# The last FFN by halves of its hidden width, and a second value group in columns form, in a four-layer decode kernel

## The chip, the cores and the metric

The kernel runs on one core of one Trainium2 chip. The metric is the device time of one execution in microseconds (us). PE is the matmul engine, PEld its weight loads, DVE the vector engine, ACT the scalar engine, SP the engine that issues the loads. "Clock" is the share of its full clock that PE was granted.

## The reference, cut to what matters

Two attention layers with a key and value cache and two gated FFNs alternate, for one new token of each of four sequences:

```python
B, Sq, D = 4, 1, 512
Hq, Hkv, Sk, Dh = 32, 8, 8192, 128        # caches: 4 x 8 x 8192 x 128, bf16, two of them
F = 1792
def _B_ref(x, w_gate, w_up, w_down):
    g = _silu(x @ w_gate)
    u = x @ w_up
    return (g * u) @ w_down
x = x + _A_ref(_layernorm(x), ...)        # attention
x = x + _B_ref(_layernorm(x), ...)        # FFN
x = x + _A_ref(_layernorm(x), ...)
x = x + _B_ref(_layernorm(x), ...)
```

The two caches hold 134 MB and are needed by both attention layers. The kernel keeps little of them on the chip and loads most of them twice: some 257 MB in all, the weights included.

## The kernel before

Everything is a step of a plan. A small simulation inside the kernel (`Plan.run`) assigns each step a start by estimated durations, and the program is then emitted in that order. Three rules of it matter here: which step an engine takes, how the estimate of a PE step grows when its instruction stream crosses a block of 256, and that a group's output projection (`oproj`) ranks by the place of the group's second load.

```python
# Plan.run: of the steps of one engine, the one ready when it comes free; ties by prio
at = max(t, free_at[e])
k = (at > free_at[e] + 1e-9, at if at > free_at[e] + 1e-9 else 0.0, s.prio[0])
...
# Plan.run.fetched: an estimate of instruction fetch, at most one block of 256 per 6 us
for k in range(first // self.PAGE_N + 1, pe_n // self.PAGE_N + 1):
    there = at + s.us * (k * self.PAGE_N - first) / s.n
    at += max(0.0, page_at + self.PAGE - there)
    page_at = max(there, page_at + self.PAGE)
```

A value group multiplies the softmax weights by two loads of 1 MB of values. In rows form that is 16 matmuls of 256 columns per load, then a 128x256 transpose and a reduction on DVE. In columns form it is 32 matmuls of 4 columns per load, and the result needs neither.

```python
direct = (l, b, g) in late_groups          # LATE = (6, ): group 6, last sequence, last attention
# rows:    matmul(out[32n:32n+32, 0:256], lhsT=p[:, 32 columns], rhs=v[:, 8 rows, 32 of 128])
# columns: matmul(out[:, 0:4],            lhsT=v[:, 128 of one row], rhs=p[:, 4 columns])
def nm():
    if not direct:
        e.transpose(blk, blk); e.tensor_reduce(osum[:], diag, AX.X, ALU.add)
    e.tensor_tensor(oT[...], got, invL[...], ALU.mult)
...
return prev, oproj(l, g, [n, ...], prios[1])
```

The FFN: 56 gate matmuls, two times 28 up matmuls, then silu over the whole width, the product with each half of up, and two times 28 down matmuls.

```python
gate = ffn_mm(wg_sb, "wg", 0, FO, [cen], tag + "g")              # FO = 14, 4 matmuls each
ups = [...]                                                      # two halves
# a1 gs = gate * rstd            DVE
# a2 eneg = exp(-gs)             ACT
# a3 us = gs * rstd              DVE
# a4 us = us / (1 + eneg)        DVE: add, reciprocal, multiply
# a5 hT[half] = us[half] * up[half]   DVE, twice
# dn: 28 down matmuls for each half
```

## Time and profile before

| | before |
|---|---|
| median of the first 3 runs | 640.53 us (639.56 to 641.21) |
| profiled span | 637.9 us |
| loads | 257 MB, 403 GB/s, DMA row at 9 or 8 in 39 of 40 slices |
| from the last long load wait to the end | 624.11 to 637.9, 13.8 us |

The lines of the page and of the timeline that carry this stand in the prediction below. They are read in two steps: the stream of loads up to about 624 us, and what PE and DVE still have to do after that. I call that stretch the tail.

- **A**: from the end of the last long load wait on PE to the first add after the projections (before: 624.11 to 628.70, 4.59 us),
- **B**: from the first gate matmul to the first down matmul (630.26 to 633.74, 3.48 us),
- **C**: from that wait's end to the end of the last vector copy (624.11 to 635.99 + 0.21 = 636.20, 12.09 us).

Two lines of DVE's timeline in the kernel before, which the prediction doesn't show: the last step of the value group's result in rows form, and the first add.

```profile
627.43 0.17 DVE L777 TENSOR_TENSOR oT<-osum,invL 128x4 bf16<-128x4 f32 x1
628.70 0.17 DVE L861 TENSOR_TENSOR xx<-xx,ps 128x16 f32<-128x16 f32 x1 [0.90 <-PE ps L709]
```

### The profile page before, as it was taken

The page shows a single profiled execution, that of the slowest core. Times are in us where ns is not written, and L with a number is a line of the kernel's source. Part 1 is how long each engine was busy: PE and PEld are TensorE (multiplying, and loading weights), DVE is VectorE, ACT ScalarE, POOL GpSimd, SP SyncE. Part 2 cuts the span into 40 slices and gives each one's busy share as a digit, 9 for nine tenths or more (in the row PEclk, how much of TensorE's full clock was granted, in tenths as well). Part 3 has the DMA queues.
Part 4 walks back from the last instruction along what each step waited for, and adds up shares of the span by engine and source line. Part 5 has one row for each costly group of instructions (what it writes and reads, how often), then busy time and mean ns, then how long its engine had stood idle before and what let it go on. Part 6 is the DMA issues. An engine that isn't in the chain of part 4 may idle for free.

```text
span 637.9 us, 18599 instructions
## 1 busy us (share of the span) xinstructions
PE 401.5 (63%) x8657; PEld 202.0 (32%) x8657; DVE 405.2 (64%) x612; ACT 40.2 (6%) x106; POOL 1.8 (0%) x8
## 2 busy tenths in 40 slices
PE   0376454375686655678565575677656776866676
PEld 0231221123542131145331241343421244721355
DVE  6386853464236958776579765466667864499732
ACT  1000200002000020000100100000100020000200
POOL 1000000000000000000000000000000000000000
PEclk9985585565556686665677677567585578577685
DMA  8999999999989999999999999999999999999991
GB/s 362 420 418 407 407 418 420 418 421 400 388 354 422 420 418 420 421 418 404 417 414 418 420 419 421 419 409 411 417 420 420 403 420 420 420 416 420 421 415 42
DMA packets 41124, 257.31 MB, mean 403 GB/s; under 512 B 3924, under 2 KB 9816, under 8 KB 11096
## 3 DMA queue, kind: packets, MB, share of 16 engines
q1 hardware_dynamic: 41048, 256.14, 97.8%
q8 instruction: 67, 1.10, 0.7%
q14 instruction: 9, 0.07, 0.0%
HBM read 256.12 MB, written 0.00 MB: 402 GB/s over the span
## 4 chain that ended last, share of the span: by engine, by line
DMA 64%; PE 16%; DVE 13%; SPq 3%; issue 2%; ACT 0%
DMA pool<-in_A_k_cache_dram 45%; DMA pool<-in_A_v_cache_dram 12%; DVE pool L589 9%; PE ps L605 8%; DMA wq_sb<-in_A_k_cache_dram 5%; PE ps L746 4%; SPq L92 3%; DMA wq_sb<-in_A_v_cache_dram 3%; PE ps L467 1%; DVE negm L624 1%; DVE wq_sb L589 1%; PE ps L792 1%; PE ps L664 1%; PE ps L845 1%; DVE ps L773 1%
## 5 line engine op out<-in xcount | busy, mean ns | idle before, releaser
L589 DVE STREAM_TRANSPOSE pool<-pool 128x2048 uint32<-128x2048 uint32 x116 | 267.1, 2308 | 88.4 <-DMA pool<-in_A_k_cache_dram 87.9
L605 PE MATMUL ps<-pool,qpad 32*32 32x512 bf16 x3840 | 197.4, 548 | 130.8 <-DVE pool L589 125.6
L605 PEld LDWEIGHTS ps<-pool,qpad 32*32 32x32 bf16 x3840 | 55.5, 110 | 248.4 <-DVE pool L589 185.8
L746 PE MATMUL ps<-pool,pp 128*32 128x256 bf16 x1952 | 100.5, 362 | 37.6 <-DMA pool<-in_A_v_cache_dram 28.9
L746 PEld LDWEIGHTS ps<-pool,pp 128*32 128x32 bf16 x1952 | 56.2, 120 | 76.3 <-DMA pool<-in_A_v_cache_dram 34.9
L773 DVE STREAM_TRANSPOSE ps<-ps 128x256 f32<-128x256 f32 x63 | 28.8, 457 | 67.4 <-PE ps L746 67.1
L628 ACT ACTIVATE pp<-ps,negm 128x512 bf16<-128x512 f32 x32 | 21.6, 686 | 322.8 <-DVE negm L624 300.5
L709 PE MATMUL ps<-oT,wo_sb 128*128 128x4 bf16 x640 | 22.4, 166 | 11.3 <-DVE oT L777 8.4
L709 PEld LDWEIGHTS ps<-oT,wo_sb 128*128 128x128 bf16 x640 | 20.0, 102 | 24.8 <-DVE oT L777 15.8
L624 DVE TENSOR_REDUCE negm<-ps 128x1 f32<-128x512 f32 x32 | 19.9, 683 | 12.4 <-PE ps L605 12.4
L467 PE MATMUL ps<-xnT,wq_sb 128*128 128x4 bf16 x640 | 18.3, 166 | 12.8 <-DMA wq_sb<-in_A_wq_dram 11.5
L467 PEld LDWEIGHTS ps<-xnT,wq_sb 128*128 128x128 bf16 x640 | 17.7, 104 | 15.3 <-DMA wq_sb<-in_A_wq_dram 11.6
L589 DVE STREAM_TRANSPOSE wq_sb<-wq_sb 128x2048 uint32<-128x2048 uint32 x8 | 18.5, 2312 | 1.8 <-DMA wq_sb<-in_A_k_cache_dram 1.8
L605 PE MATMUL ps<-wq_sb,qpad 32*32 32x512 bf16 x256 | 11.8, 492 | 9.1 <-DVE wq_sb L589 9.1
L664 PE MATMUL ps<-ident,pp 128*128 128x128 bf16 x128 | 15.4, 300 | 2.5 <-DVE oT L777 1.1
L453 ACT ACTIVATE lnv<-var,eps_sb 128x4 f32<-128x4 f32 x10 | 3.0, 297 | 221.5 <-DVE var L448 221.5
L664 PEld LDWEIGHTS ps<-ident,pp 128*128 128x128 bf16 x128 | 11.9, 137 | 9.6 <-DVE selw L684 2.9
L775 DVE TENSOR_REDUCE osum<-ps 128x4 f32<-128x32 f32 x63 | 12.1, 192 | 2.2
L777 DVE TENSOR_TENSOR oT<-osum,invL 128x4 bf16<-128x4 f32 x63 | 10.6, 169 | 2.1
L673 ACT ACTIVATE pp<-ps 128x1024 bf16<-128x1024 bf16 x8 | 8.2, 1024 | 30.1 <-PE ps L664 30.1
L845 PE MATMUL ps<-hT,wd_sb 128*128 128x4 bf16 x280 | 8.6, 166 | 1.8 <-issue 1.1
L653 DVE TENSOR_SCALAR pp<-pp,alpha 128x512 bf16<-128x512 bf16 x32 | 9.0, 344 | 1.1 <-ACT alpha L646 1.1
(68 smaller groups left out, 143.4 us busy)
## 6 DMA issues: line engine op xcount, KB each, us to landing
pool<-in_A_k_cache_dram SPq DMA_DIRECT2D x116, 1024.0 KB, 10.2
pool<-in_A_v_cache_dram SPq DMA_DIRECT2D x101, 1024.0 KB, 10.8
wq_sb<-in_A_k_cache_dram SPq DMA_DIRECT2D x8, 1024.0 KB, 14.8
wq_sb<-in_A_v_cache_dram SPq DMA_DIRECT2D x5, 1024.0 KB, 16.2
wq_sb<-in_A_wq_dram SPq DMA_DIRECT2D x1, 4096.0 KB, 20.0
wo_sb<-in_A_wo_dram SPq DMA_DIRECT2D x4, 1024.0 KB, 15.5
wg_sb<-in_B_w_gate_dram SPq DMA_DIRECT2D x2, 896.0 KB, 19.2
wu_sb<-in_B_w_up_dram SPq DMA_DIRECT2D x2, 896.0 KB, 16.9
```

The source lines that it names most:

```text
L92: ins = self.eng[engname].dma_start(out_ap, in_ap)
L467: op("pe", lambda e: e.matmul(ps[:, bk * BW + h * B:bk * BW + (h + 1) * B], lhsT=wq_sb[:, kt, h * Dh:(h + 1) * Dh], rhs=xnT[:, kt * B:(kt ...
L589: op("dve", lambda e: e.transpose(v, v), reads=keys, writes=keys)
L605: op("pe", lambda e: e.matmul(ps[32 * c:32 * (c + 1), a * BW:(a + 1) * BW], lhsT=qpad[rows, qbuf, es_, g, :], rhs=ap[h][rows, :, es_ // 2, ...
L624: op("dve", lambda e: e.tensor_reduce(negm[:, q, a:a + 1], bank(a), AX.X, ALU.max, negate=True), reads=[f"pb{a}"], writes=[f"negm{q}_{a}"])
L628: op("act", lambda e: e.activation(pblk(q)[:, :, a, :], bank(a).rearrange("p (t j) -> p t j", j=32), ACTF.Exp, bias=negm[:, q, a:a + 1], s ...
L664: op("pe", lambda e: e.matmul(stg[:, t * P:(t + 1) * P], lhsT=pp[:, q, blk * P:(blk + 1) * P], rhs=ident[:], is_transpose=True, start=True ...
L709: op("pe", lambda e: e.matmul(ps[:, OPJ * BW + nq * B:OPJ * BW + (nq + 1) * B], lhsT=wo_sb[:, h, nq * P:(nq + 1) * P], rhs=oT[:, l, h, :], ...
L746: op("pe", lambda e: e.matmul(ps[32 * n:32 * (n + 1), bk * BW:bk * BW + 256], lhsT=pp[:, q, col:col + 32], rhs=v[:, 8 * f:8 * (f + 1), 32 ...
L773: op("dve", lambda e: e.transpose(blk, blk), reads=[f"pb{bk}"], writes=[f"pb{bk}"])
L775: op("dve", lambda e: e.tensor_reduce(osum[:], diag, AX.X, ALU.add), reads=[f"pb{bk}"], writes=["osum"])
L845: op("pe", lambda e: e.matmul(ps[:, bk * BW + nq * B:bk * BW + (nq + 1) * B], lhsT=wd_sb[:, fo, nq * P:(nq + 1) * P], rhs=hT[:, fo * B:(fo ...
```

## The change

Its intent: let the last FFN's silu begin when half of the gate is there, so that it is finished when PE comes to the down projection; and spare a further late value group the transpose and reduction after its matmuls.

```diff
-LATE = (6, )
+LATE = (6, 3)
...
-            gate = ffn_mm(wg_sb, "wg", 0, FO, [cen], tag + "g")
+            parts = 2 if dst is not None else 1        # dst: the last FFN only
+            for k in range(parts):
+                gates.append(ffn_mm(wg_sb, "wg", k * FO // parts, (k + 1) * FO // parts,
+                                    [cen] + gates[-1:], f"{tag}g{k}"))
...
+            for k in range(parts):
+                cs = slice(k * FO * B // parts, (k + 1) * FO * B // parts)
                 # a1, a2, a3, a4 as before, on columns cs alone
+                silu.append(PL.add("dve", 0.98 if parts == 1 else 0.65, a4, [e_, r_], CHAIN))
...
-                hs_ = PL.add("dve", 0.2, a5, [s, ups[h]], CHAIN, free=f"{tag}u{h}")
+                hs_ = PL.add("dve", 0.2, a5, [silu[h * parts // 2], ups[h]], CHAIN, free=f"{tag}u{h}")
```

## The prediction

> **What bounds the kernel now.** I read the page from the top: engine shares and slices, the DMA queue, the chain that ended last, and then, because the diff touches only the end of the program, the timeline of the last 30 us.
>
> ```profile
> PE 401.5 (63%) x8657; PEld 202.0 (32%) x8657; DVE 405.2 (64%) x612; ACT 40.2 (6%) x106; POOL 1.8 (0%) x8
> DMA  8999999999989999999999999999999999999991
> q1 hardware_dynamic: 41048, 256.14, 97.8%
> DMA 64%; PE 16%; DVE 13%; SPq 3%; issue 2%; ACT 0%
> ```
>
> No compute engine is above 64%, the DMA row is at 9 from the second slice to the last but one, and the data queue fills 97.8% of the span. 257 MB at 403 GB/s is the kernel; nothing that the diff does before the last load lands can be worth anything. The last DMA slice (622 to 638) reads 1, so there is a compute tail there. Its timeline and the waits say what it consists of:
>
> ```profile
> 619.49 0.55 PE L709 MATMUL ps<-oT,wo_sb 128*128 128x4 bf16 x16
> 624.11 1.05 PE L746 MATMUL ps<-wq_sb,pp 128*32 128x256 bf16 x16 [4.07 <-DMA wq_sb<-in_A_v_cache_dram]
> 625.09 0.59 PE L709 MATMUL ps<-oT,wo_sb 128*128 128x4 bf16 x16
> 625.61 1.04 PE L746 MATMUL ps<-pool,pp 128*32 128x256 bf16 x16
> 626.59 1.01 PE L731 MATMUL ps<-pp,pool 128*128 128x4 bf16 x32
> 627.65 1.01 PE L709 MATMUL ps<-oT,wo_sb 128*128 128x4 bf16 x32
> 629.13 0.64 PE L433 MATMUL ps<-xx,onesm 128*128 128x32 f32 x2 [0.47 <-DVE xx L428]
> 630.26 1.65 PE L792 MATMUL ps<-xnT,wg_sb 128*128 128x4 bf16 x56 [0.49 <-DVE xnT L442]
> 631.78 1.63 PE L792 MATMUL ps<-xnT,wu_sb 128*128 128x4 bf16 x56
> 633.74 1.65 PE L845 MATMUL ps<-hT,wd_sb 128*128 128x4 bf16 x56 [0.33 <-DVE hT L837]
> ```
>
> PE waits 4.07 us for a value load (one of the last three), then works almost without a gap to the end. From 624.11 to the span's end at 637.9 are 13.8 us, 2.2% of the span. That is all the change can work on. In it PE is the bound; its own idle time is 0.47 and 0.49 us around the layer norm (untouched) and 0.33 us in front of the down projection, named in the waits as DVE hT.
>
> ```profile
> 631.95 0.22 DVE L812 TENSOR_TENSOR gs<-ps,rstd 128x56 f32<-128x56 f32 x1 [1.48 <-PE ps L792]
> 632.21 0.25 ACT L817 ACTIVATE eneg<-gs 128x56 f32<-128x56 f32 x1 [1.16 <-DVE gs L812]
> 632.49 0.19 DVE L826 TENSOR_SCALAR eneg<-eneg 128x56 f32<-128x56 f32 x1
> 632.71 0.50 DVE L828 RECIPROCAL eneg<-eneg 128x56 f32<-128x56 f32 x1
> 633.25 0.22 DVE L829 TENSOR_TENSOR us<-us,eneg 128x56 f32<-128x56 f32 x1
> 633.50 0.28 DVE L837 TENSOR_TENSOR hT<-us,ps 128x28 bf16<-128x28 f32 x2
> ```
>
> This is that wait: silu starts only when all 56 gate matmuls are done, and takes 1.79 us to the first down matmul, against about 1.5 us of up matmuls.
>
> **What the Trainium skill says.** "Perfetto Trace Analysis", Roofline: one trn2 core alone may pull about 120% of its 358 GB/s share, bounded near 435 GB/s. The trace agrees (403 mean, 420 in most slices): the stream has no slack to win. "VectorE: DVE Perf Modes", on the TRN2 errata: a small vector operation pays a fixed cost per instruction, so halving the operand doesn't halve the time. The trace agrees: 217 ns for 128x56 (L812), 180 ns for 128x28 (L837). "TensorE: Matmul & The Clock Gate", Part 1: the array falls to half its clock after an idle window of about 3.4 us, and start to start never drops below about 25 ns however few the columns. The trace agrees on both: the granted clock is 1.00 at 618 to 620 us and 0.50 from 621 us on, after the wait for the load; and the 56 gate and 56 up matmuls run at (633.41 - 630.26 - 0.17) / 111 = 26.9 ns each.
>
> **The change, part one: the FFN in halves.** The matmuls stay 56 + 56 + 56; only the last FFN is split, the three earlier ones lie under the stream and keep one part. Durations of a half, interpolated between measured widths: tensor_tensor 0.18 (L837 itself), exp 0.23 (0.205 at width 4, 0.250 at 56), tensor_scalar 0.175 (0.155 and 0.193), reciprocal 0.335 (0.36 at width 32, 0.503 at 56). Hand-overs of 0.03 to 0.05 us as in the fence.
> - Gate half 0 ends 27 x 0.027 + 0.17 = 0.89 after 630.26, at 631.15; rstd was ready at 631.04, so it doesn't hold it. Scaling starts 631.19, exp 631.41, the group of three 631.67 to 632.42 (0.175 + 0.335 + 0.18 and hand-overs).
> - Half 1 of the gate is done at 631.9 but its scaling queues behind that: 632.43 to 632.61; exp to 632.88; meanwhile the second rstd multiplication to 632.80.
> - Up half 0 is done at 632.66, so hT half 0 can be made 632.82 to 633.00, and the group of three for half 1 runs 632.99 to 633.75, hT half 1 to 633.95.
> - PE issues its last up matmul at 630.26 + 111 x 0.0269 = 633.25. hT half 0 has been there since 633.06, so down half 0 follows without a wait at about 633.28, and takes 0.75. Down half 1 needs hT half 1 at 634.01, when PE reaches it at 634.03.
> Sum: down starts at 633.28 in place of 633.74, a gain of **0.46 us**. DVE gets six more instructions (about +0.9 us of busy time), but works on them where it stood idle for 1.48 us before.
>
> **Part two: value group 3 in columns form.** It removes one 128x256 transpose (0.47), one reduction (0.19) from DVE, and turns 2 x 16 matmuls of 256 columns into 2 x 32 of 4. At the halved clock 16 row matmuls hold PE 0.98 us (624.11 to 625.09, 625.61 to 626.59); 32 column ones hold it about 32 x 0.0272 = 0.87 (L731, spacing (1.01 - 0.17) / 31). That is 0.11 saved twice, **0.2 us** of PE time. The removed DVE work (626.70 to 627.60) lay beside L731, which ended at 627.60, so it was hidden: the chain names it only by a tie.
>
> But the order changes. The kernel's scheduler takes, among the steps ready when PE comes free, the one whose load stands first in the queue. In the kernel before, group 3's output projection became ready only after both halves of the last load had been multiplied. Now it is ready one DVE step of 0.17 us after its matmuls, while PE does the first half of the last load; its load stands ahead of the last one, so I expect it between the halves. Then the second half ends the group alone, and PE must wait for one DVE multiplication before the last 16 projections: 0.04 + 0.17 + 0.05 plus the drain of a matmul, some 0.3 in all. Followed through: 624.11 + 0.87 + 0.47 + 0.87 + 0.44 + 0.46 + 0.44 = 627.66, drain to 627.82, DVE to 628.03, projection 628.08 to 628.65, against 628.66 before. The gain of part two is **0.0**, within 0.15 either way.
>
> **Sum:** 640.53 - 0.46 - 0.0 = about 640.1 us, a gain of 0.07%.
>
> **Rivals.**
> 1. *The DVE order defeats the split.* All these steps have one priority; if up half 0 is expected a little later than half 1's exp, hT half 0 goes behind the group of three of half 1 and PE gets it only at 633.9: a loss of 0.15 in place of the gain, 640.7. For it: by my reckoning they are 0.1 us apart. Against it: the order of readiness I worked out has hT first.
> 2. *The columns form pays in full.* If the projection of group 3 runs after both halves as before, it hides the DVE step, and part two gives about 0.2: 639.9.
> 3. *Instruction fetch.* 64 more PE instructions shift where its stream crosses a block; the trace has PE gaps called issue up to 0.95 us (554.89), under the full stream. In the tail the DMA is nearly idle and no PE wait there is put down to issue, so I give it little: at worst 641.
> 4. *The transfer hides it.* If the last load landed later than PE reaches it now, faster compute would only wait. The DMA share is 0.06 at 625.5 to 626 and 0.00 after; PE comes to the last load's second half at about 627.2. So no.
>
> **Range and chances.** The effect is a fraction of a microsecond; the runs of the kernel before spread over 639.56 to 641.21. The range of 639.0 to 641.2 is that spread moved down by 0.3 and widened a little. Two per cent would be 12.8 us, nearly the whole tail of 13.8 us, so a verdict other than "same" would need the stream itself to change, and no load, slot or order before the tail is touched.
>
> **What would show it.** Right: gate and up matmuls without a gap; no DVE wait before L845, whose first matmul comes 3.0 us after the first gate matmul (before: 3.48); one L773 less; 64 matmuls of L731 more; the time from the last load wait's end to the first add after the projection (4.6 us before) unchanged within 0.15; span from that wait's end to the end 13.3 us in place of 13.8. Wrong: a wait for DVE before L845 that stays or grows, a gap between up halves, an issue gap in the tail, or a stretch of the stream before 620 us that differs, which would be variation and not the change.

## The result, and the profile after

Median 639.48 us over 4 runs (638.67 to 640.59), against 640.87 us over 4 runs of the kernel before (639.56 to 641.52). The ratio is 0.9982, with a 95% interval of 0.9957 to 1.0007.

The page after says the same of the stream as the page before (shares of the engines, the DMA row, the data queue):

```profile
PE 397.2 (62%) x8689; PEld 201.8 (32%) x8689; DVE 405.1 (64%) x615; ACT 40.4 (6%) x107; POOL 1.8 (0%) x8
DMA  8999999999989999999999999999999999999991
q1 hardware_dynamic: 41048, 256.14, 97.9%
```

PE has 32 matmuls more (64 in columns form for 32 in rows form) and DVE three instructions more: five from the split, two less from the columns form. Compared instruction by instruction, the two programs are alike on every engine up to the group of the last load wait. PE's timeline of the tail after the change (start, length, line, tiles, count, and in brackets the idle time before and its cause; short lines left out):

```profile
623.74 1.01 PE L727 MATMUL ps<-pp,wq_sb 128*128 128x4 bf16 x32 [3.13 <-DMA wq_sb<-in_A_v_cache_dram]
624.61 0.57 PE L705 MATMUL ps<-oT,wo_sb 128*128 128x4 bf16 x16
625.03 1.42 PE L727 MATMUL ps<-pp,pool 128*128 128x4 bf16 x48
626.32 0.57 PE L705 MATMUL ps<-oT,wo_sb 128*128 128x4 bf16 x16
626.74 0.57 PE L727 MATMUL ps<-pp,pool 128*128 128x4 bf16 x16
627.57 0.58 PE L705 MATMUL ps<-oT,wo_sb 128*128 128x4 bf16 x16 [0.26 <-DVE oT L773]
629.76 1.66 PE L788 MATMUL ps<-xnT,wg_sb 128*128 128x4 bf16 x56 [0.50 <-DVE xnT L438]
631.27 1.63 PE L788 MATMUL ps<-xnT,wu_sb 128*128 128x4 bf16 x56
632.77 1.63 PE L852 MATMUL ps<-hT,wd_sb 128*128 128x4 bf16 x56
```

Two things are to be seen. The down projection (L852) has no wait before it any more: B is 632.77 - 629.76 = 3.01 us. And the projections stand where the prediction put them, one between the halves of the last load and one behind, with a new wait of 0.26 us for DVE before the last. A is 628.19 - 623.74 = 4.45 us, C is 635.21 - 623.74 = 11.47 us. So the tail gave 12.09 - 11.47 = 0.62 us: 0.47 from the FFN, 0.14 from the value part. The medians differ by 1.39; the rest can't come from the tail.

DVE's timeline after the change, cut to the first add and the lines of the FFN that are used below:

```profile
628.19 0.17 DVE L868 TENSOR_TENSOR xx<-xx,ps 128x16 f32<-128x16 f32 x1 [0.68 <-PE ps L705]
630.71 0.19 DVE L817 TENSOR_TENSOR gs<-ps,rstd 128x28 f32<-128x28 f32 x1 [0.74 <-PE ps L788]
632.20 0.18 DVE L844 TENSOR_TENSOR hT<-us,ps 128x28 bf16<-128x28 f32 x1
632.34 0.18 DVE L832 TENSOR_SCALAR eneg<-eneg 128x28 f32<-128x28 f32 x1
633.14 0.18 DVE L844 TENSOR_TENSOR hT<-us,ps 128x28 bf16<-128x28 f32 x1
```

hT of half 0 is done at 632.38, 0.4 us before PE asks for it; hT of half 1 at 633.32, while PE reaches its matmuls at about 632.77 + 28 x 0.027 = 633.53. The third and fourth lines are worth remembering: hT of half 0 stands ahead of the group of three (L832 to L835) of half 1.

### The profile page after: what moved, and what is told of

The parts are those of the page before. It is cut to its first block, busy times and chain, and to the rows that moved or that the text cites. A ratio compares the mean times of both kernels' runs of the same rounds, so it can differ in the third digit from the quotient of the medians.

```text
span 636.9 us, 18667 instructions
## 1 busy us (share of the span) xinstructions
PE 397.2 (62%) x8689; PEld 201.8 (32%) x8689; DVE 405.1 (64%) x615; ACT 40.4 (6%) x107; POOL 1.8 (0%) x8
## 4 chain that ended last, share of the span: by engine, by line
DMA 66%; PE 15%; DVE 12%; SPq 3%; issue 2%
DMA pool<-in_A_k_cache_dram 44%; DMA pool<-in_A_v_cache_dram 13%; DVE pool L585 10%; PE ps L601 8%; DMA wq_sb<-in_A_v_cache_dram 5%; DMA wq_sb<-in_A_k_cache_dram 4%; PE ps L742 3%; SPq L92 3%; PE ps L463 1%; PE ps L788 1%; DVE wq_sb L585 1%; DVE ps L769 0%; PE ps L852 0%; PE ps L727 0%; PE ps L705 0%
## 5 line engine op out<-in xcount | busy, mean ns | idle before, releaser
L601 PE MATMUL ps<-pool,qpad 32*32 32x512 bf16 x3840 | 193.2, 537 | 128.3 <-DVE pool L585 124.7
L742 PE MATMUL ps<-pool,pp 128*32 128x256 bf16 x1936 | 98.8, 359 | 46.7 <-DMA pool<-in_A_v_cache_dram 36.5
L671 DVE COPY pp<-ps 128x1024 bf16<-128x1024 bf16 x8 | 5.5, 690 | 6.8 <-PE ps L660 6.8
```

The source lines that it names most:

```text
L601: op("pe", lambda e: e.matmul(ps[32 * c:32 * (c + 1), a * BW:(a + 1) * BW], lhsT=qpad[rows, qbuf, es_, g, :], rhs=ap[h][rows, :, es_ // 2, ...
L742: op("pe", lambda e: e.matmul(ps[32 * n:32 * (n + 1), bk * BW:bk * BW + 256], lhsT=pp[:, q, col:col + 32], rhs=v[:, 8 * f:8 * (f + 1), 32 ...
```

## The experiments

My theory after the first result: the gain of the change is the 0.62 us of the tail, made of two independent parts, and the rest of the difference of medians is variation of the stream. Rivals: the parts depend on one another; the stream itself became faster; the orders on DVE or PE are what matters, and not the split or the form as such. Of each run I give A, B and C from its trace and the ratio to the kernel before in the same rounds.

| run | A | B | C | ratio (95% interval) |
|---|---|---|---|---|
| before, first trace | 4.59 | 3.48 | 12.09 | |
| null_before | 4.60 | 3.47 | 12.11 | 0.9998 (0.9983 to 1.0013) |
| after, first trace | 4.45 | 3.01 | 11.47 | 0.9982 (0.9957 to 1.0007) |
| after_again | 4.46 | 3.01 | 11.48 | 0.9992 (0.9979 to 1.0004) |
| ffn_only | 4.59 | 3.49 | 12.11 | 1.0002 (0.9988 to 1.0016) |
| ffn_pinned | 4.59 | 3.01 | 11.61 | 0.9985 (0.9969 to 1.0002) |
| late_only | 4.46 | 3.48 | 11.96 | 0.9989 (0.9969 to 1.0008) |
| dve_swapped | 4.46 | 3.49 | 11.98 | 1.0002 (0.9982 to 1.0022) |
| proj_last | 4.04 | 3.01 | 11.06 | 0.9969 (0.9956 to 0.9981) |
| proj_last_2 | 4.03 | 3.01 | 11.04 | 0.9972 (0.9957 to 0.9986) |
| three_last | 4.35 | 3.01 | 11.37 | 0.9977 (0.9964 to 0.9990) |
| proj_last_pad | 4.04 | 3.01 | 11.85 | 0.9986 (0.9972 to 1.0001) |

**How small a difference can be told: null_before and after_again.** The first is the kernel before, unedited, run as though it were changed; the second is the changed kernel, unedited.

> The kernel before, submitted as if it were a change. Both theories (tail shortened by 0.6 us and the rest of the 1.4 us of medians is variation of the stream; or the change also speeds up the stream) expect a ratio of 1.000 whose interval shows how small a difference five rounds can tell: about 0.2% either way. Tail from the end of the last load wait to the end of the last vector copy 12.1 us, as before.

> The changed kernel again. Theory (the whole gain lies in the tail): ratio 0.999, within 0.9975 to 1.0005; last load wait's end to last copy's end 11.5 us (before 12.1); first gate matmul to first down matmul 3.0 us (before 3.5); the wait's end to the first add after the projection 4.45 us (before 4.6). Rival (the stream itself gained): the last load wait ends 0.7 us or more earlier than in the null run, in this trace and the first one alike, and the ratio is 0.998 again.

Five rounds tell 0.15%, that is 1 us. The tail lengths repeat within 0.02 us. The ratio of the changed kernel fell back to 0.9992, where 0.62 us of 640 make 0.9990, and its last load wait ended at 625.10, later than the 623.74 of its first trace. So these runs show no gain of the stream; the first 0.9982 held some luck.

**The FFN part alone: ffn_only.**

```diff
-LATE = (6, 3)
+LATE = (6, )
```

> FFN in halves, group 3 left in rows form. Theory: first gate to first down matmul 3.0 us as in the changed kernel, the wait's end to the first add 4.6 us as before; last wait's end to last copy's end 11.6 us, that is 0.47 of the 0.62. Rival (the two parts help each other, or the value part gives the gain): 3.0 us does not come, or the sum is over 11.8.

A miss: nothing was gained at all, C is 12.11. The split is there, and the down projection waits as before:

```profile
630.81 1.66 PE L788 MATMUL ps<-xnT,wg_sb 128*128 128x4 bf16 x56 [0.49 <-DVE xnT L438]
634.30 1.65 PE L852 MATMUL ps<-hT,wd_sb 128*128 128x4 bf16 x56 [0.34 <-DVE hT L844]
```

DVE's timeline of the same run says why. The last three steps before the down projection are these:

```profile
633.60 0.33 DVE L834 RECIPROCAL eneg<-eneg 128x28 f32<-128x28 f32 x1
633.96 0.19 DVE L835 TENSOR_TENSOR us<-us,eneg 128x28 f32<-128x28 f32 x1
634.07 0.30 DVE L844 TENSOR_TENSOR hT<-us,ps 128x28 bf16<-128x28 f32 x2
```

Both hT products stand at the end, x2 in one line. That of half 0 could have been made when its up matmuls were done, but it now queues behind half 1's reciprocal. It is the first rival of the prediction. That a change of the value part decides it looks odd, until one prints the start times that the kernel's own plan assigned. In the changed kernel the plan holds hT half 0 to be ready at 626.614 + 0.06 = 626.67, ahead of half 1's group of three at 626.692 + 0.06 = 626.75. Without the 64 more PE instructions of the columns form, a block of 256 ends in the second gate half, the plan adds 0.12 us there, and the order is 626.48 for hT against 626.45 for the group. These are numbers of the plan and not of the chip, and they differ by 0.03 us; but the program follows them.

**The order alone: ffn_pinned and dve_swapped.** The first repairs ffn_only by an estimate (the plan takes half 1's exponential for slower than it is); the second spoils the whole change by a dependency. Neither touches any other instruction of PE, DVE or ACT.

```diff
 # ffn_pinned, on top of ffn_only
-                e_ = PL.add("act", 0.25, a2, [s], CHAIN)
+                e_ = PL.add("act", 0.25 + 0.25 * k, a2, [s], CHAIN)
 # dve_swapped, on top of the changed kernel
-  hs_ = PL.add("dve", 0.2, a5, [silu[h * parts // 2], ups[h]], CHAIN, ...)
+  hs_ = PL.add("dve", 0.2, a5, [silu[-1], silu[h * parts // 2], ups[h]], CHAIN, ...)
```

> FFN in halves without the value part, with hT half 0 put ahead of the second half's group of three again (in the run ffn_only it had fallen behind, and first gate to first down matmul stayed at 3.49). Theory (that one place in the vector engine's order is the whole difference): 3.01 us and no wait of PE before the down projection; the wait's end to the first add 4.59; last wait to last copy 11.6. Rival (the columns form itself is needed for the FFN gain, say through the clock or the fetch of instructions): 3.4 to 3.5 remains.

> The whole change, with only hT half 0 moved behind the second half's group of three. Theory: first gate to first down matmul goes back from 3.01 to 3.49 us with a PE wait of about 0.34 for DVE, last wait to last copy 11.95. Rival (the vector order is neutral, ffn_only lost its gain otherwise): 3.0 stays.

Both as the theory expected: 3.01 with hT ahead, 3.49 with it behind, whatever the value part is. First PE in ffn_pinned, with no wait before the down projection:

```profile
630.86 1.65 PE L788 MATMUL ps<-xnT,wg_sb 128*128 128x4 bf16 x56 [0.49 <-DVE xnT L438]
633.87 1.63 PE L852 MATMUL ps<-hT,wd_sb 128*128 128x4 bf16 x56
```

And PE in dve_swapped, with the wait back:

```profile
631.51 1.66 PE L788 MATMUL ps<-xnT,wg_sb 128*128 128x4 bf16 x56 [0.50 <-DVE xnT L438]
635.00 1.65 PE L852 MATMUL ps<-hT,wd_sb 128*128 128x4 bf16 x56 [0.35 <-DVE hT L844]
```

One place in DVE's order is the whole worth of the FFN part. What remains of the split without it is nothing: B is then 3.49 where the unsplit FFN has 3.48, because the second half's chain ends no earlier than the whole one did (hT is complete 634.37 - 630.81 = 3.56 us after the first gate matmul in ffn_only, and 633.78 - 630.26 = 3.52 us after it in the kernel before).

**The value part alone: late_only.**

```diff
-            parts = 2 if dst is not None else 1
+            parts = 1
```

> Columns form for group 3 with the FFN whole. Theory: the wait's end to the first add 4.45 as in the changed kernel, first gate to first down matmul 3.48 as before, last wait to last copy 11.95: the value part alone is worth 0.14 us. Rival (it needs the FFN split): 4.6.

A is 4.46 as in the changed kernel, B 3.48, C 11.96: 0.13 us by itself. With ffn_pinned's 0.48 that makes 0.61 of the 0.62. Once the order is right, the parts simply add.

**The order of the projections: proj_last, twice.** Group 3's projection gets the last rank, so that it stands behind the second half of the last load, as before the change.

```diff
-  return prev, oproj(l, g, [n, ...], prios[1])
+  return prev, oproj(l, g, [n, ...],
+                     prios[1] if (l, b, g) != (1, B - 1, 3) else [900])
```

> The changed kernel with the projection of group 3 behind the second half of the last load in place of between the halves. Theory (the second vector multiplication is exposed by 0.26 us of PE wait plus its drain): the wait before the last 16 projections vanishes and the wait's end to the first add falls from 4.45 to about 4.1 us, last wait to last copy 11.1. Rival (PE has other costs there, the order is neutral): 4.35 to 4.5. The whole time can show neither: 0.4 us is 0.06%.

> The order with both projections last, again, because its ratio of 0.9969 in five rounds is twice what its tail can explain (12.1 down to 11.06 us is 0.16%). Theory (the tail is all): last wait to last copy 11.06 again, and a ratio of 0.9984 within the interval of 0.13% seen on the null run. Rival (the stream is faster too): 0.997 again with the last wait ending over 1 us earlier than in kernels of the same call.

PE's timeline of proj_last has the 64 column matmuls and the 32 projections in one piece each, and no wait between:

```profile
626.45 1.85 PE L727 MATMUL ps<-pp,pool 128*128 128x4 bf16 x64
628.15 0.99 PE L705 MATMUL ps<-oT,wo_sb 128*128 128x4 bf16 x32
```

A falls by 0.42 us to 4.03 to 4.04: the wait of 0.26 and the drain before it are covered by 16 matmuls that had to be done anyway. Of the versions that ran at the clock of 0.50, this one has the shortest tail. In the rounds that it shared with after_again, all its six runs (638.10 to 639.66) lie under all six of the other (640.04 to 640.89), and its ratio to the kernel before is under 1 with its whole interval. The size isn't explained, though: a tail shorter by 1.03 to 1.05 us makes 0.9984, and 0.997 was seen twice. The rival put on record for the second run, a faster stream, asked for a last wait that ends over 1 us earlier than in kernels of the same call. That did not come: it ended at 624.72, against 624.70 in ffn_pinned, 623.98 in late_only and 625.48 in dve_swapped.

**Is that program's stream faster? proj_last_pad.** The same kernel with five needless vector instructions at the end.

```diff
   op("dve", lambda e: e.tensor_copy(xlast, ...), ...)
+  for i in range(4):
+      op("dve", lambda e: e.tensor_scalar(m2[:], m2[:], 1.0, None, op0=ALU.mult), ...)
+  op("dve", lambda e: e.tensor_copy(xlast, ...), ...)
```

> proj_last with five needless vector instructions at its end, about 1.0 us, so that its tail is as long as that of the kernel before (12.1). Theory A (the ratios of 0.997 of proj_last owed half to chance): ratio 1.000. Theory B (that program's stream of loads is really some 0.8 us faster, tail apart): ratio 0.9985 to 0.9990. An interval of 0.13% will only just tell these apart.

Inconclusive. The padding came to 0.8 us (C 11.85), so the tail alone would give 0.9996; 0.9986 was measured, and its interval holds both answers. It leans to Theory B, and three_last below, with the same order of projections, lies as far under what its tail explains (0.9977 against 0.9989). Against a faster stream stand the traces: the last wait ended at 625.14 in proj_last, and at 625.10, 625.32 and 624.65 in the changed kernel, the null run and ffn_only. Nor does the program differ there: compared instruction by instruction, proj_last and the changed kernel are alike on every engine until 2.58 us after that wait's end (626.32 in the trace of the changed kernel). This stays open.

**Rows and columns at two clocks: warm_columns and warm_rows.** Twelve needless matmuls of 512 columns are put in the load wait, so that the granted clock is high for what follows. The second kernel has group 3 in rows form (and with it ffn_only's order in the FFN, which is not read here). One look each, state unknown; only stages are read.

```diff
+  def warm():
+      for i in range(12):
+          op("pe", lambda e: e.matmul(ps[:, 0:BW], lhsT=ident[:], rhs=pp[:, q, 0:BW], ...), ...)
```

> The changed kernel with 12 needless matmuls of 512 columns in PE's wait for the last loads, to raise the granted clock (they may run past the landing, so only what follows them is read). Theory (32 column matmuls are bound by issue, not by the clock): 0.87 us to the projection as at half clock, at most 0.05 less.

> The same needless matmuls with group 3 in rows form. Theory (row matmuls are slow in the tail because the clock is halved): if the granted clock reads 1.00 there, 16 row matmuls take 0.45 to 0.55 us to the projection in place of 0.98, half of what columns take, and the columns form would lose. Rival (rows are slow for another cause, such as data just landed): 0.9 or more at full clock. If the clock stays 0.50, the run tells nothing.

PE's timeline of warm_rows, from the load wait on (two lines left out before the last):

```profile
624.37 0.62 PE L751 MATMUL ps<-wq_sb,pp 128*32 128x256 bf16 x16 [0.77 <-DMA wq_sb<-in_A_v_cache_dram]
624.92 0.55 PE L705 MATMUL ps<-oT,wo_sb 128*128 128x4 bf16 x16
626.86 0.56 PE L734 MATMUL ps<-pp,pool 128*128 128x4 bf16 x16 [0.35 <-DMA pool<-in_A_v_cache_dram]
```

The clock read 1.00 in both runs from 624 to 628 us (in warm_rows it had done so since 619.4 us, before the needless matmuls began at 621.06). There, 16 row matmuls hold PE for 624.92 - 624.37 = 0.55 us instead of 0.98, as the theory said, and 32 column matmuls 0.81 instead of 0.87, which is 0.06 less where the theory allowed 0.05. So a load in columns form costs PE more at full clock and less at half clock, and the tail ran at 0.50 in all twelve traces without needless matmuls.

Which form makes the shorter tail at full clock isn't shown. With rows A is 3.90 us, even though PE now came too early for the last half of the last load and waited 0.35 us for it. With columns (warm_columns) A is 4.24 us, but there the projection of group 3 stands between the halves; less the 0.42 us that proj_last gained by its order, that would be 3.8 us, an estimate. In warm_rows the last half was there 626.86 - 624.37 = 2.49 us after the end of the first wait; its landing is the next limit.

**One more group in columns form: three_last.** On top of proj_last.

```diff
-LATE = (6, 3)
+LATE = (6, 3, 5)
```

> Projections of groups 3 and 6 last, as in proj_last, and group 5 in columns form too, which lets its 16 projection matmuls go ahead of the last load wait instead of behind it. Theory (only what stands behind the wait on PE counts, 0.42 us for 16 projections): the wait's end to the first add 3.62 us, last wait to last copy 10.62 (proj_last 11.05). Rival (columns form is slower per load and moves the wait's end): the same 4.04, or a later end of the wait.

A miss that is instructive: A is 4.35, not 3.62, and worse than proj_last's 4.04. PE's timeline:

```profile
623.05 0.85 PE L705 MATMUL ps<-oT,wo_sb 128*128 128x4 bf16 x26 [1.60 <-issue]
624.70 1.01 PE L727 MATMUL ps<-pp,wq_sb 128*128 128x4 bf16 x32 [0.80 <-DMA wq_sb<-in_A_v_cache_dram]
625.58 1.42 PE L727 MATMUL ps<-pp,pool 128*128 128x4 bf16 x48
627.19 0.59 PE L727 MATMUL ps<-pp,pool 128*128 128x4 bf16 x16 [0.19 <-DMA pool<-in_A_v_cache_dram]
627.64 0.30 PE L705 MATMUL ps<-oT,wo_sb 128*128 128x4 bf16 x6
628.16 0.85 PE L705 MATMUL ps<-oT,wo_sb 128*128 128x4 bf16 x26 [0.23 <-issue]
```

Group 5's projection did move ahead of the wait. Then PE came to the last half before it had landed (again 627.19 - 624.70 = 2.49 us after the first wait's end; proj_last reaches it about 2.58 us after). And twice PE stopped for nothing that the profile shows, for 1.60 us before the wait and for 0.23 us in the tail. Against proj_last the 64 matmuls of the last two loads take 0.36 us more (627.64 - 625.58 = 2.06 in place of 1.70), and the way from there to the first add 0.38 us more (1.41 in place of 1.03): together what was missed (4.35 - 3.62 = 0.73). Between the two stops lie 26 + 32 + 48 + 16 + 6 = 128 matmuls with as many weight loads, 256 PE instructions, which is the block in which, by the Trainium skill ("Runtime: NRT & Kernel Launch", Instruction fetch mechanics), instructions are fetched. The same spacing is found across kernels: counted in the traces, the last stop of this kind before the tail stands in front of the 8269th matmul in before, after, after_again, ffn_only, late_only and proj_last (0.19 to 0.33 us), and the two of three_last in front of the 8397th and the 8525th, 128 and 256 further on. But the other eleven timed traces pass these two without a stop. That the stops are fetches is an inference from the spacing; no run took the fetch away.

## Why the prediction was right, and where it was not

The time, 639.48 us, lies 0.6 us under the 640.1 predicted and inside the range. Four runs can't resolve such a distance (the same kernel's median in after_again was 640.49); the lengths of the tail are the fair test.

- **The bound, and that only the tail can gain:** right, though the DMA row has one 8 among the 9s that were read. The page after has the same stream, and the ratio of 0.9992 in after_again is what the tail explains.
- **Part one, 0.46 us:** measured 0.47, by the way it was worked out. Down followed the first gate matmul after 3.01 us (predicted 3.02). hT half 1 came 0.2 us before PE needed it, not just in time: the hand-overs between independent DVE instructions are shorter than I took them (L817 of half 1 starts at 631.87, 0.11 us after the 0.19 us long L835 of half 0, which I had end to start with a gap).
- **The six more DVE instructions:** they were five; hT was already made in two.
- **The clock of 0.50 in the tail:** right in size, and so in all twelve traces. What the prediction gave as its cause, an idle time of the array before, the traces don't bear out: before the change the clock fell at 620.9 us, 0.9 us into the wait; after it, at 614.7 us, with PE busy in 2.65 of the 3.41 us before. No run shows what lowers it.
- **Part two, 0.0 within 0.15:** 0.14, at the edge. The projection did go between the halves, and the wait behind it came (0.26 us on PE). The mis-sized terms are the two projections of 16 matmuls that lie before the second half, 0.42 us each and not 0.47 and 0.46 (together 0.09); the other 0.05 are the column matmuls (48 in 1.29 us, I had 1.31) and the drain (0.61 from the second half's first matmul to the vector step, I had 0.64). The step exposed behind the second half was called "some 0.3 in all"; the prediction's own sum has 0.42 for it (627.66 to 628.08), and the trace 0.40 (626.74 + 16 x 0.0266 = 627.17 to 627.57).
- **"The removed DVE work lay beside L731, which ended at 627.60, so it was hidden":** wrong, and it is why part two was sized at 0.2 at best. 627.60 is the modelled end of the last matmul; at the spacing of 0.027 us PE was ready for the next one at 626.59 + 32 x 0.0272 = 627.46, and began the projections at 627.65, after the transposed result. So about 0.19 us of the transpose, reduction and multiplication were exposed. The Trainium skill says it ("Perfetto Trace Analysis", Tensor Engine Instruction: the end of a matmul in the profile is an estimate), and proj_last agrees: there 64 column matmuls from 626.45 at (1.85 - 0.17) / 63 = 0.0267 us each are through at 628.16, and the projections start at 628.15.
- **Rival 1, the order on DVE:** named, and given little weight, for the program at hand rightly. But the step "the order of readiness I worked out has hT first" hides how narrow it was: 0.08 us in the plan, and with the value part left out the order tips the other way and the gain is gone. The loss it would bring was oversized too: PE gets going at 3.49 us after the first gate matmul, no later than before, where I had put it 0.15 later.
- **Rival 2, "part two gives about 0.2" with both projections last:** it gives 4.59 - 4.03 = 0.56 us. The 0.2 of shorter matmuls is there; the transpose of the point above adds 0.19; and the projection of group 5 holds PE 0.43 us where column matmuls follow it, against 0.52 where row matmuls did (625.09 to 625.61 before), another 0.09. These make 0.5 of the 0.56. They are read stage by stage from the traces of before and proj_last; no run took them apart.
- **Rival 3, instruction fetch:** no such stop in the tail of the changed kernel; with 64 further instructions, in three_last, one stop before the last load wait and one in the tail.
- **Rival 4, the landing:** right for the change, where PE reaches the last half 3.00 us after the first wait's end against a landing at 2.49; but only 0.1 us is left in proj_last.

## What to carry to other kernels

When loads fill 97% of the time, read from the timeline how long the tail after the last load is before weighing a compute change: here 13.8 us of 640, so no rearrangement in it can be a two per cent matter. Splitting a chain to overlap it is worth what the consumer's first half needs, and only if that half's last step isn't queued behind the other half's work on an in-order engine; look at the built order and pin it. And judge two forms of a matmul at the clock that the stage is granted: in the time that they held PE, the same two forms changed places between 0.50 and 1.00.

## What the Trainium skill lacked or had wrong

- "TensorE: Matmul & The Clock Gate", Part 1, gives about 3.4 us of sustained activity as what raises the clock. In warm_columns the granted clock fell from 1.00 to 0.50 at 629.0 us, although PE had been busy for 3.15 of the 3.41 us before, with matmuls of 4 columns alone. It stayed at 0.50 from the first gate matmul on (630.75 to 635.40), where PE was busy for 4.64 of 4.65 us with 168 such matmuls. So by this trace busy time of narrow matmuls neither held nor raised the clock; the page doesn't say so.
- The same page gives issue gaps by number of columns, but none measured at both clocks for the two forms compared here: 16 matmuls of 256 columns with 32 weight columns each held PE 0.98 us at clock 0.50 and 0.55 at 1.00, 32 of 4 columns with 128 weight columns 0.87 and 0.81.
- "Runtime: NRT & Kernel Launch", Instruction fetch mechanics, calls the cost of crossing a block mostly hidden. In three_last two stops 256 PE instructions apart took 1.60 us while the loads still ran and 0.23 us after them, if these stops are fetches.
